# Two transformer layers on one core: spare matmuls behind the opening are left out of the stream of TensorE

## The chip, the core and the metric

The kernel runs on one core of one Trainium2 chip. Five engines work side by side, each through its own list of instructions in order: TensorE (PE in the profile; PEld is its weight load), VectorE (DVE), ScalarE (ACT), GpSimd (POOL) and SyncE (SP), which issues the transfers. They wait for one another through semaphores. The metric is the device time of one execution in microseconds (us); lower is better. The profile also records the share of its full clock that TensorE was granted, and this share is part of the story told here.

## The reference

`x` is 2048 tokens by 512 channels in bf16. The network is attention, MLP, attention, MLP with the same weights twice, each on a layer-normalised input and added back:

```python
def _A_ref(x, wqkv, wo):                       # 32 heads of 16 channels
    q, k, v = ...                              # x @ wqkv, split and reshaped
    scores = einsum("bhqd,bhkd->bhqk", q, k) * 16 ** -0.5
    o = einsum("bhqk,bhkd->bhqd", softmax(scores), v)
    return o.reshape(B, S, D) @ wo
def _B_ref(x, w1, b1, w2, b2):                 # 512 -> 1792 -> 512
    return gelu(x @ w1 + b1) @ w2 + b2

x = x + _A_ref(_layernorm(x), wqkv, wo)
x = x + _B_ref(_layernorm(x), w1, b1, w2, b2)
x = x + _A_ref(_layernorm(x), wqkv, wo)
x = x + _B_ref(_layernorm(x), w1, b1, w2, b2)
```

Per layer there are 32 heads of 2048 by 2048 scores, so the exponentials (134 million per layer) are a large part of the work, and the products have an inner size of only 16.

## The kernel before, in words

**Tiles.** The queries are worked in chunks of 512; a pass is one chunk, a group of heads in four strips of 32 channels, and a run of key tiles of 128. A score cell is one key tile by 512 queries for one strip: a matmul with 32 active rows (two heads, one of them masked to zero in the queries) and 128 columns (L1588, `score`), which lands in one of eight PSUM banks. Up to four cells with different row positions run beside each other in the array.

**Exponentials.** A part of the cells is exponentiated by ScalarE straight out of PSUM, two or three banks in one instruction (L2238, `exps`). PSUM banks 0 to 4 form two slots for it, later six banks: while one slot is read, the other is filled. The rest of the cells goes to VectorE (L1855, `dfirst`), which writes scaled integers; GpSimd (L2101, `shift`) adds constants to them so that the bits read as bf16 are terms of the exponential.

**The product with the values** (L2305, `pvs`): four matmuls of 128 rows by 17 columns beside each other in the array, the 17th column being the row sum, accumulated in bank 6 (`PVB`). A DVE transpose and a division close each pass (L1067 and after).

**Projections and MLP** (L706, `quads`): four matmuls of 32 output columns beside each other. GELU is done by ScalarE in a long instruction over half of the hidden layer (L1267), with a table load before and after.

**The order.** Nothing is scheduled on the chip. At build time, `_Sched.run` plays the whole program through with estimated durations: threads (generators) offer operations, the one that could start first is taken, its instructions are appended to its engine's list (`_Prog.group`), the waits that its reads and writes ask for are put ahead of it (`_dep_waits`), and the engine's planned clock is moved on. `_Prog.emit` then writes the lists out. All engines are therefore in a fixed order, and the durations on the chip only decide how long each wait lasts.

**Spare matmuls.** Before each operation of TensorE, `_Sched.fill` looks at the planned gap up to it. `active` keeps a running mean, over the last 3.4 planned us (`WINDOW`), of how many of four 32-wide strips of the array are at work. As long as the gap holds one more operation and this mean is under 2.3 of 4 (`WARM`), `fill` asks `free` for a PSUM bank that nobody needs at that moment and `filler` for a spare operation: four matmuls of `B2row` with itself (L1576), 512 columns long, written into that bank, whose contents nobody reads; or, into the bank of the open value product, four with zero weights. A spare operation counts 0.213 us in the plan. Its event is kept in `fills`, so that `free` knows that the bank holds nothing of worth.

## Time and profile before

| | us |
|---|---|
| three runs of the kernel | 1415.38, 1415.41, 1416.63 (median 1415.41) |
| the profiled execution, whole | 1417.29 |
| its span, first to last instruction | 1415.4 |
| DVE busy | 1265.5 (89%) |
| ACT busy | 1388.6 (98%) |
| POOL busy | 1006.8 (71%) |

The span is the part of the profiled execution that the trace covers; 1.9 us lie around it. Engine times in the profile are unions of instruction spans. For TensorE such a span contains the pipeline's latency, so that a stretch can look full although the array streams only for part of it; the number of matmuls in a stretch tells more. One instruction of L1576 is one of four matmuls that run beside each other.

A stretch in the table of windows shows: its bounds, its length, the busy time of the engine with the number of instructions in brackets (each one that lies in the stretch at least in part), the granted clock of TensorE as a share of full speed, the mean busy share of the DMA engines, and what they moved in GB/s.

### The profile page before, as it was taken

How to read it: one execution, taken by the hardware profiler on the slowest of the kernel's cores; microseconds unless marked ns; L12 is line 12 of the kernel's file. 1: busy time of each engine (PE TensorE's matmuls, PEld its weight loads, DVE VectorE, ACT ScalarE, POOL GpSimd, SP SyncE). 2: the span in 40 equal slices, each digit the busy share in tenths (PEclk: the TensorE clock that was granted, in tenths of full speed). 3: DMA queues.
4: the chain of work that ended last, by engine and by line, in shares of the span. 5: the costliest groups of instructions: out<-in, count | busy, mean ns of one | idle time of the engine just before them, and what ended most of it. 6: DMA issues, size and time to landing. Idle time of an engine off the chain costs nothing.

```text
span 1415.4 us, 45657 instructions
## 1 busy us (share of the span) xinstructions
PE 1387.9 (98%) x19382; PEld 415.4 (29%) x19382; DVE 1265.5 (89%) x2482; ACT 1388.6 (98%) x1392; POOL 1006.8 (71%) x1257
## 2 busy tenths in 40 slices
PE   8999999999999999999999999999999999999999
PEld 3222222222222222222222222222222222344345
DVE  8999999979999899998998899999888978899884
ACT  7999999999999999999999999999999999999995
POOL 0489778757787678766877779647776776877661
PEclk9999999999999999999999999999999999999999
DMA  5200001123121340214312141101133112311121
GB/s 149 65 2 1 2 2 32 41 89 101 44 54 39 98 106 24 59 41 124 81 39 54 54 121 53 47 16 32 39 102 95 31 35 91 111 17 40 28 72 42
DMA packets 122308, 80.41 MB, mean 57 GB/s; under 512 B 36732, under 2 KB 121084, under 8 KB 122108
## 3 DMA queue, kind: packets, MB, share of 16 engines
q1 hardware_dynamic: 122108, 77.49, 19.7%
q8 instruction: 156, 2.56, 0.7%
q14 instruction: 44, 0.36, 0.1%
HBM read 65.67 MB, written 4.19 MB: 49 GB/s over the span
## 4 chain that ended last, share of the span: by engine, by line
PE 60%; ACT 28%; DVE 9%; POOL 2%; DMA 1%; issue 0%; ACTq 0%; DVEq 0%
ACT pt L2238 24%; PE ps L2305 22%; PE ps L1588 20%; PE ps L706 18%; ACT v L2238 2%; DVE dp L1855 2%; DVE kt L1855 1%; ACT g L1267 1%; ACT q L2238 1%; POOL dp L2101 1%; DVE stats L839 1%; DVE xf L1855 0%; POOL kt L2101 0%; DVE xt L1067 0%; PE ps L1576 0%; DVE xln L870 0%
## 5 line engine op out<-in xcount | busy, mean ns | idle before, releaser
L2238 ACT ACTIVATE pt<-ps 128x1024 bf16<-128x1024 f32 (+1 forms) x1170 | 1160.4, 1123 | 5.5 <-PE ps L1588 4.9
L2101 POOL INT64_ADD dp<-dp x760 | 618.1, 825 | 181.0 <-DVE dp L1855 40.3
L1588 PE MATMUL ps<-qp,kt 32*128 32x512 bf16 x4096 | 543.8, 384 | 9.5 <-ACT pt L2238 4.1
L1855 DVE TENSOR_SCALAR dp<-ps 128x512 uint16<-128x512 f32 x762 | 509.4, 681 | 48.9 <-PE ps L1588 43.8
L1588 PEld LDWEIGHTS ps<-qp,kt 32*128 32x128 bf16 x4096 | 138.8, 91 | 566.5 <-ACT pt L2238 158.4
L2305 PE MATMUL ps<-dp,vc 128*17 128x512 bf16 (+1 forms) x2574 | 288.7, 357 | 0.9 <-POOL xp L2101 0.2
L2305 PE MATMUL ps<-pt,v 128*17 128x512 bf16 (+1 forms) x2810 | 272.7, 359 | 2.5 <-POOL dp L2101 0.7
L2101 POOL INT64_ADD kt<-kt x255 | 205.2, 811 | 89.9 <-DVE kt L1855 43.1
L1855 DVE TENSOR_SCALAR kt<-ps 128x512 uint16<-128x512 f32 x254 | 171.6, 683 | 27.2 <-PE ps L1588 24.7
L706 PE MATMUL ps<-xf,wr 128*32 128x512 bf16 (+1 forms) x1888 | 131.9, 367 | 1.8 <-DMA xf<-xln 1.7
L2305 PE MATMUL ps<-dp,v 128*17 128x512 bf16 (+1 forms) x858 | 123.9, 357 | 3.8 <-DVE xt L1067 2.2
L2305 PE MATMUL ps<-kt,vc 128*17 128x512 bf16 (+1 forms) x948 | 125.1, 340 | 0.3 <-POOL kt L2101 0.2
L2101 POOL INT64_ADD v<-v x111 | 91.5, 831 | 39.2 <-DVE v L1855 18.1
L706 PE MATMUL ps<-wr,g 128*32 128x512 bf16 x1408 | 104.2, 383 | 0.3 <-DMA wr<-in_B_w_dram 0.3
L2305 PEld LDWEIGHTS ps<-dp,vc 128*17 128x17 bf16 x2574 | 77.0, 89 | 66.9 <-issue 34.4
L2101 POOL INT64_ADD xf<-xf x74 | 59.6, 805 | 49.1 <-DVE xf L1855 31.8
L2305 PEld LDWEIGHTS ps<-pt,v 128*17 128x17 bf16 x2810 | 67.7, 88 | 79.8 <-issue 54.2
L1855 DVE TENSOR_SCALAR v<-ps 128x512 uint16<-128x512 f32 x112 | 75.9, 684 | 13.1 <-PE ps L1588 12.0
L1249 DVE TENSOR_SCALAR g<-ps,hb1t 128x512 bf16<-128x512 f32 (+1 forms) x112 | 79.1, 706 | 7.6 <-PE ps L706 7.5
L2305 PE MATMUL ps<-kt,v 128*17 128x512 bf16 (+1 forms) x440 | 68.1, 351 | 0.4 <-DVE v L1063 0.4
L2238 ACT ACTIVATE kt<-ps 128x1024 bf16<-128x1024 f32 (+1 forms) x61 | 59.7, 1057 | 0.1
L2238 ACT ACTIVATE v<-ps 128x1024 bf16<-128x1024 f32 (+1 forms) x55 | 55.6, 1078 | 0.1
(127 smaller groups left out, 1436.7 us busy)
## 6 DMA issues: line engine op xcount, KB each, us to landing
wr<-in_B_w_dram SPq DMA_DIRECT2D x174, 256.0 KB, 2.9
wr<-in_A_wqkv_dram SPq DMA_DIRECT2D x24, 256.0 KB, 3.1
x<-in_A_x_dram SPq DMA_DIRECT2D x7, 512.0 KB, 4.0
wr<-in_A_wo_dram SPq DMA_DIRECT2D x10, 256.0 KB, 3.2
kept<-x SPq DMA_DIRECT2D x4, 512.0 KB, 2.9
x<-kept SPq DMA_DIRECT2D x4, 512.0 KB, 4.1
out_dram<-x SPq DMA_DIRECT2D x16, 128.0 KB, 2.3
q<-in_B_w_dram SPq DMA_DIRECT2D x3, 512.0 KB, 5.0
```

The lines of the kernel that those rows point to most:

```text
L706: return [lambda e, a=a: e.matmul(out[32 * a:32 * a + 32, :], lhsT=lhsT[:, 32 * a:32 * a + 32], rhs=rhs, start=start, stop=stop, tile_posi ...
L839: yield _Op("dve", 0.66, lambda e, t=t, src=src: e.bn_stats(T["STATS"][:, t, :], src), reads=[key], writes=["ST.%d" % t], prio=prio)
L1249: yield _Op("dve", 0.21 + n / 966, lambda e, fc=fc, pb=pb: e.tensor_scalar(T["G"][:, fc, q], pb, T["HB1T"][:, fc:fc + 1], None, op0=ALU.ad ...
L1267: lambda e, g=g: e.activation(out=g, in_=g, func=ACT.Gelu_apprx_tanh), reads=gk, writes=gk, prio=2)
L1588: return (lambda e: e.matmul(o, lhsT=lhsT, rhs=rhs, start=True, stop=True, tile_position=(32 * a, 0)), ["K%d.%d.%d" % (l, gb, kt // 4), "Q ...
L1855: yield _Op("dve", 0.682, lambda e: e.tensor_scalar(u, self.bank(b), E_SCALE, E_BIAS, op0=ALU.mult, op1=ALU.add), reads=["B.%d" % b], writ ...
L2101: op = _Op("pool", PFIX + PWORD * 128 * n * (1 + both), lambda e: e.int64_add(dst, src, by * PACKED), reads=reads, writes=writes)
L2238: yield _Op("act", 0.065 + 0.4267 * n, lambda e, src=src, dst=dst: e.activation(out=dst, in_=src, func=ACT.Exp, scale=0.25), reads=["B.%d" ...
L2305: op.fns.append(lambda e, o=o, lhsT=q[0][0][m], rhs=q[0][1][:, n * m:n * m + n], a=a, st=st, sp=sp: e.matmul(o, lhsT=lhsT, rhs=rhs, start= ...
```

## The change

From a planned time of 60 us on, `fill` does all that it did, but does not append the four matmuls: the waits that they would have needed are still put into TensorE's list, the planned clock still moves on by 0.213 us, and the bank is marked as holding nothing. As the plan's clocks are the same, every later decision is the same too. TensorE's list loses 416 matmuls and nothing else; its waits, and the lists of the other four engines, are unchanged in number and order.

```diff
+FILLED = 60
...
             op = self.filler(b, mode)
             self.mode = mode
-            ev = self.P.group("pe", op.fns, op.reads, op.writes)
-            if b != PVB:
-                self.fills.add(ev)
+            if self.clock["pe"] < FILLED:
+                ev = self.P.group("pe", op.fns, op.reads, op.writes)
+                if b != PVB:
+                    self.fills.add(ev)
+            else:
+                self.P._dep_waits("pe", op.reads, op.writes)
+                ev = None
+                if b != PVB:
+                    self.P.lastw.pop("B.%d" % b, None)
+                    self.P.reads["B.%d" % b] = {}
             self.note(now + into, now + into + MM + cold, op)
             self.ops.append(("pe", now, into + MM + cold, "FILL"))
             self.clock["pe"] = now + into + MM + cold
-            self.end[ev] = self.clock["pe"] + LATENCY["pe"]
+            if ev:
+                self.end[ev] = self.clock["pe"] + LATENCY["pe"]
```

`_dep_waits` writes an engine's waits for the last writers and readers of the named buffers; `lastw` and `reads` are the tables in which those are kept, and clearing a bank in them means that its next user has nothing to wait for on its account.

## The prediction

> **What bounds the kernel now.** I read the page first, then the chain of waits, then the table of windows, then the timeline where the granted clock dips.

> ```profile
> PE 1387.9 (98%) x19382; PEld 415.4 (29%) x19382; DVE 1265.5 (89%) x2482; ACT 1388.6 (98%) x1392; POOL 1006.8 (71%) x1257
> PE 60%; ACT 28%; DVE 9%; POOL 2%; DMA 1%; issue 0%; ACTq 0%; DVEq 0%
> 30.00:1080.00 1050.00, 1036.04 (x13487) 281.84 (x13487) 962.35 (x1846) 1048.36 (x1048) 776.70 (x968) 1.00 0.20 55
> 1095.00:1390.00 295.00, 290.07 (x4905) 106.91 (x4906) 255.76 (x477) 294.64 (x286) 216.08 (x267) 1.00 0.19 53
> ```

> The first two rows show TensorE and ScalarE both at 98%, and the chain that ended last running 60% on TensorE and 28% on ScalarE. The two window rows (PE, PEld, DVE, ACT, POOL in this order) sharpen it: from 30 to 1080 us ScalarE sat idle for 1050 - 1048.36 = 1.64 us, from 1095 to 1390 us for 295 - 294.64 = 0.36 us. So the two engines are tied: whatever delays TensorE soon starves ScalarE, but whatever speeds TensorE up can win back at most those 2.0 us, because ScalarE has no more idle time to give.

> The second thing to see is the clock. This trace holds one dip, and it is an experiment made for us:

> ```profile
> 1082.78:1086.20 3.42, 1.47 (x22) 1.00 0.53 131
> 1086.20:1089.61 3.41, 3.41 (x30) 0.50 0.37 112
> 1089.61:1093.02 3.41, 3.41 (x51) 1.00 0.11 43
> 171.43:174.84 3.41, 3.20 (x35) 1.00 0.03 7
> ```

> ```profile
> 1086.14 1.04 PE L706 MATMUL ps<-xf,wr 128*32 128x512 bf16 x8 [1.73 <-DMA xf<-xln]
> ...
> 1087.65 1.04 PE L706 MATMUL ps<-xf,wr 128*32 128x512 bf16 x8
> ...
> 1090.13 0.39 PE L1588 MATMUL ps<-qp,kt 32*128 32x512 bf16 x3
> ...
> 1091.00 0.39 PE L1588 MATMUL ps<-qp,kt 32*128 32x512 bf16 x3
> ```

> ```profile
> 1087.77 1.02 ACT L2238 ACTIVATE pt<-ps 128x1024 bf16<-128x1024 f32 x1 [2.06 <-PE ps L1588]
> 1089.70 1.94 ACT L2238 ACTIVATE pt<-ps 128x1024 bf16<-128x1024 f32 x2 [0.92 <-PE ps L1588]
> ```

> TensorE waited 1.73 us for a transfer, so the stretch 1082.78 to 1086.20 held only 22 matmuls. In the next 3.41 us it was granted half its clock, then the full clock again. So the clock is judged by stretches of 3.41 us: 22 matmuls were too few, and a stretch of 35 (171.43) kept the clock whole. Somewhere between lies the limit.

> The price: a projection of eight matmuls with a score group of three takes 1087.65 - 1086.14 = 1.51 us at half clock and 1091.00 - 1090.13 = 0.87 us at full clock. A half-clock stretch of a fully loaded TensorE thus does 3.41 / 1.51 x 0.87 = 1.97 us of work and loses 1.44 us. The counts agree: 30 matmuls against 51 right behind, (51 - 30) x 3.41 / 51 = 1.40 us. ScalarE lost 2.06 + 0.92 = 2.98 us over the place, 1.25 us more than the stall of 1.73.

> **The change part by part.** It removes 416 matmuls, and nothing else moves: no DMA, wait or instruction of another engine.

> ```profile
> 60.00:1416.00 1356.00, 33.87 (x416) 1.00 0.19 54
> 239.69:243.11 3.42, 1.22 (x16) 1.00 0.48 80
> 519.58:523.00 3.42, 1.00 (x12) 1.00 0.64 207
> 915.53:918.94 3.41, 1.39 (x24) 1.00 0.01 2
> 918.94:922.36 3.42, 0.52 (x8) 1.00 0.00 0
> 970.14:973.56 3.42, 1.09 (x16) 1.00 0.41 82
> 973.56:976.97 3.41, 0.13 (x4) 1.00 0.02 6
> 1151.05:1154.46 3.41, 2.09 (x32) 1.00 0.02 5
> 1154.46:1157.87 3.41, 2.15 (x40) 1.00 0.00 0
> 1157.87:1161.29 3.42, 0.34 (x8) 1.00 0.00 0
> ```

> These are the windows of L1576 alone. The 33.87 us of span that the spares cover are no saving: nobody reads their banks, and they stand where the plan saw TensorE wait. What they can have delayed is the operation right behind them, and that gain is capped by ScalarE's 2.0 us above. I take 0.6 us, a third, between 0 and 2.0; below nothing it cannot go but through the clock, since no work that remains reads their banks.

> The other side is the clock. The same stretches with all of TensorE's matmuls:

> ```profile
> 239.69:243.11 3.42, 3.02 (x42) 1.00 0.48 80
> 243.11:246.52 3.41, 3.40 (x42) 1.00 0.39 77
> 519.58:523.00 3.42, 3.19 (x40) 1.00 0.64 207
> 523.00:526.41 3.41, 3.41 (x48) 1.00 0.48 140
> 915.53:918.94 3.41, 3.20 (x44) 1.00 0.01 2
> 918.94:922.36 3.42, 3.42 (x46) 1.00 0.00 0
> 970.14:973.56 3.42, 3.08 (x46) 1.00 0.41 82
> 973.56:976.97 3.41, 3.09 (x40) 1.00 0.02 6
> 1151.05:1154.46 3.41, 3.04 (x39) 1.00 0.02 5
> 1154.46:1157.87 3.41, 2.79 (x45) 1.00 0.00 0
> 1157.87:1161.29 3.42, 2.92 (x48) 1.00 0.00 0
> ```

> All are cut on the grid of the dip. Subtract the spares: 239.69 keeps 42 - 16 = 26 matmuls, 519.58 keeps 28, 915.53 keeps 20, 970.14 keeps 30, 1151.05 keeps 7 and 1154.46 keeps 5.

> *Step 1, sure by the row of the dip.* 1151.05 and 1154.46 fall far below 22. ScalarE is in a GELU there and takes no scores:

> ```profile
> 1148.61 6.27 ACT L1267 ACTIVATE g<-g 128x3584 bf16<-128x3584 bf16 x2
> ```

> The clock halves at 1154.46 and stays halved until a busy stretch has passed, to 1161.29. The stretch 1157.87 has 48 - 8 = 40 matmuls to do where 30 fit: 10 x 3.41 / 51 = 0.67 us; the 5 matmuls of 1154.46 take 5 x 0.067 = 0.3 us longer. Together 1.0 us, on the path, because ScalarE resumes on these scores.

> *Step 2, by the limit.* A half-clock stretch costs what does not fit behind it: (n - 30) x 3.41 / 51, n being the matmuls of the next stretch, nothing if n is under 30, at most 1.4. So 239.69 costs nothing (26 follow in 243.11, which at half clock are a full stretch and keep the next one whole); 519.58 costs 18 x 0.067 = 1.2 us; 915.53 (38 follow) 0.54; 970.14 (36 follow) 0.40. The mean is 0.54; two of the stretches not shown have followers as full as 1089.61, so I take 0.65 us, between 0 and 1.4.

> How many there are hangs on the limit between 22 and 35. I measure it against a stretch that streams without a break:

> ```profile
> 1154.03 0.83 PE L1576 MATMUL ps<-b2row 128*32 128x512 bf16 x12
> ...
> 1155.20 1.48 PE L1576 MATMUL ps<-b2row 128*32 128x512 bf16 x24
> ```

> Twelve more matmuls took 0.65 us, so 3.41 us hold 63 at most. I take half of that, 31, as the limit: an estimate that lies inside the bracket. On this grid eleven stretches with 512-column matmuls, the first 239.69 and the last 970.14, hold 20 to 30 without spares; two of them are covered, as 243.11 is, by a dip that the stretch before them set off. So nine dips, 9 x 0.65 = 5.9 us. Three more low stretches after 1235 us mix in 256-column matmuls, where the count misleads; they stay in the upper range.

> The sum: + 1.0 + 5.9 - 0.6 = + 6.3 us. The profiled execution took 1417.29 us (span 1415.4), 1.9 above the median of 1415.41; the sum carries over, so **1421.7 us**. No row says where the grid lies in another execution; the count is for one position of it.

> [...]

> **The rivals.**

> *Few dips (0.32).* The limit lies just above 22, so 26 to 30 matmuls keep the clock. Then step 1 and 915.53 remain at most: + 1.0 + 0.5 - 0.6 = + 0.9, at least + 0.4: 1415.8 to 1416.3 us. For it: the only row of a dip is at 22 with a pause of 1.73 us, and without spares most pauses are shorter. Against: nothing between 22 and 35 was seen whole either.

> *Many dips (0.16).* The limit lies just under 35: some sixteen dips, with the three after 1235 us, at 0.9: + 14.4 + 1.0 - 0.6 = + 14.8, 1430 us.

> *TensorE gains (0.04).* Spares stand in the chain of waits:

> ```profile
> by line: PE ps L2305 32.7%; PE ps L1588 27.1%; ACT pt L2238 18.5%; PE ps L1576 8.7%; PE ps L706 5.5%; DVE dp L1855 3.5%; POOL xp L2101 3.1%; issue 1.4%; DVE nmr L854 0.9%; DVE ry L858 0.7%; PE ps L2313 0.1%
> 239.69:243.11 3.42, 3.42 (x4) 1.00 0.48 80
> ```

> The first row is the chain from 230 to 250 us: 8.7% of 20 us is 1.7 us of spares right ahead of scores. If TensorE alone set the pace there, and at two like places, the kernel would gain 5 us: 1410. It decides from the point at which ScalarE has idle time to follow; the second row, ScalarE's own window, has it busy for 3.42 of 3.42 us at the same place. So the cap of 2.0 us holds, and with no dip beyond step 1 the result would be + 1.0 - 2.0 = 1414.4, slightly faster.

> That the change does nothing is ruled out but for the size: 416 instructions are gone.

> **How the numbers follow.** Forecast (limit about 31; five to ten dips, + 3 to + 10 us) 0.48, few dips 0.32, many 0.16, gain 0.04. The range 1415.6 to 1429 leaves out the lower third of few dips, the gain and the upper half of many dips, about 0.2. A measurement of this kernel can tell some 0.2%, 2.8 us, from no change: under 1412.6 is faster (0.02), over 1418.2 slower. Same holds few dips, half of the gain and a little of the forecast: 0.36. Slower: 0.62.

> **What would show it.** In the changed kernel's windows, stretches of 3.41 us at 0.50 behind the low stretches named; each lowers the mean granted clock by 0.5 x 3.41 / 1415 = 0.0012. ScalarE's waits for L1588, beside each dip, should grow by about 1 us in all where the follower is full. The stretch at 1151 must dip: if it does not, the whole reading of the clock is wrong. If dips come and ScalarE's waits do not, step 2's price is wrong; if 915.53 (20) keeps its clock, the limit is not a count of matmuls. If the time falls by more than 2 us, the tie between the two engines is not what the first rows say.

## The result

The changed kernel took 1424.7 us (median of 4 runs, 1424.33 to 1426.52) against 1415.39 us of the kernel before (4 runs): 1.0072 times as long, interval 1.006 to 1.0085, that is 9.3 us slower by the medians. The ratio is not the quotient of the two medians, which is 1.0066; by the ratio the loss is 10.2 us. The forecast was 1421.7 us, 6.3 us slower.

In the profile of the changed kernel the lines of the code stand nine further down: L2247 is the exponential on ScalarE (L2238 before), L1597 the scores (L1588), L2314 the product with the values (L2305), L715 the projections (L706). First the page's rows and the mean granted clock:

```profile
span 1422.9 us, 44846 instructions
PE 1374.4 (97%) x18966; PEld 407.9 (29%) x18966; DVE 1266.4 (89%) x2482; ACT 1390.5 (98%) x1392; POOL 1007.3 (71%) x1257
PE 59%; ACT 30%; DVE 9%; POOL 1%; issue 1%; ACTq 0%; DVEq 0%
```

```profile
core 0: 1422.9 us, clock 0.987
```

ScalarE runs the same 1392 instructions in a span 7.5 us longer, and 416 matmuls are gone. The number that moved is the clock. A half-clock stretch of 3.41 us costs 0.5 x 3.41 / 1422.9 = 0.0012 of the mean, so 0.987 means some eleven of them. The table of windows of TensorE, cut on the grid of this execution, finds them:

```profile
633.71:637.13 3.42, 1.67 (x27) 1.00 0.27 77
637.13:640.54 3.41, 3.41 (x30) 0.50 0.02 5
640.54:643.95 3.41, 3.41 (x29) 0.50 0.00 0
643.95:647.37 3.42, 3.42 (x63) 1.00 0.42 119
917.02:920.43 3.41, 1.93 (x21) 1.00 0.01 2
920.43:923.85 3.42, 3.08 (x20) 0.50 0.02 5
923.85:927.26 3.41, 3.41 (x27) 0.50 0.00 0
934.09:937.50 3.41, 2.09 (x26) 1.00 0.02 5
937.50:940.91 3.41, 3.41 (x29) 0.50 0.00 0
954.57:957.98 3.41, 2.38 (x29) 1.00 0.00 0
957.98:961.39 3.41, 1.94 (x21) 1.00 0.00 0
961.39:964.81 3.42, 3.17 (x24) 0.50 0.02 5
964.81:968.22 3.41, 3.27 (x29) 0.50 0.19 38
968.22:971.63 3.41, 3.41 (x30) 0.50 0.00 0
1155.95:1159.37 3.42, 1.70 (x15) 1.00 0.00 0
1159.37:1162.78 3.41, 0.63 (x5) 0.50 0.00 0
1162.78:1166.19 3.41, 2.99 (x24) 0.50 0.00 0
1166.19:1169.61 3.42, 3.42 (x32) 0.50 0.02 5
1169.61:1173.02 3.41, 3.41 (x53) 1.00 0.00 0
237.77:241.18 3.41, 2.33 (x31) 1.00 0.19 38
241.18:244.59 3.41, 2.61 (x31) 1.00 0.38 77
244.59:248.00 3.41, 2.46 (x26) 1.00 0.19 38
```

There are five dips with eleven stretches: two at 637, two at 920, one at 937, three at 961, three at 1159. They lie on one grid: between the starts of the dips (637.13, 920.43, 937.50, 961.39 and 1159.37) are 283.30, 17.07, 23.89 and 197.98 us, which are 83, 5, 7 and 58 stretches of 3.41 us (283.30 / 83 = 3.413). Read the busy column ahead of each: 1.67, 1.93, 2.09, 1.94 and 1.70 us of 3.41 let the clock fall; 2.33, 2.38, 2.46 and 2.61 held it. Then read on: in four of the five dips the clock does not return after one stretch as at 1086 in the kernel before. At 920.43, 961.39, 964.81, 1159.37 and 1162.78 the half-clock stretch was itself not full (3.08, 3.17, 3.27, 0.63, 2.99), and the next stayed at half. Of the six full ones five were followed by full speed; 637.13 is the exception, full by this column and yet followed by another half.

What it costs shows on ScalarE, whose own windows over the same places are these, behind a GELU at 635 and in the dips:

```profile
643.95:647.37 3.42, 0.88 (x1) 1.00 0.42 119
920.43:923.85 3.42, 2.64 (x3) 0.50 0.02 5
923.85:927.26 3.41, 2.32 (x3) 0.50 0.00 0
961.39:964.81 3.42, 3.05 (x4) 0.50 0.02 5
964.81:968.22 3.41, 2.61 (x4) 0.50 0.19 38
968.22:971.63 3.41, 2.44 (x3) 0.50 0.00 0
1166.19:1169.61 3.42, 2.10 (x3) 0.50 0.02 5
```

Idle: 2.54 + 0.78 + 1.09 + 0.37 + 0.80 + 0.97 + 1.32 = 7.9 us. ScalarE's waits say the same in one row, the changed kernel's first and the kernel before's second (total, number, longest); the last row is TensorE's wait for the late transfer in the kernel before:

```profile
ACT pt L2247 <- PE ps L1597: 10.2, 16, 2.7
```

```profile
ACT pt L2238 <- PE ps L1588: 4.9, 6, 2.1
...
PE ps L706 <- DMA xf<-xln: 1.7, 1, 1.7
```

Of the 4.9 us before, 2.98 belonged to the transfer that was late at 1085 us and its dip; in the changed kernel's profile no such wait for xf occurs. So 10.2 - (4.9 - 2.98) = 8.3 us are new; the idle time at the dips, 7.9 us, is nearly all of that.

A second measure, which the texts below use, is the delay: how much later the changed kernel's profile starts the same instruction of ScalarE. It is 2.7 us behind the dip at 637 and 8.5 us behind the one at 961 (972.14 against 963.62 us). It falls to 5.4 us where the kernel before had its late transfer, and grows to 7.4 us behind the GELU. That makes 8.5 us for the eight stretches of the first four dips and 2.0 us for the three at the GELU, 10.5 us in all.

### The profile page after: what moved, and what is told of

Its sections match the earlier page's. It is cut to its first block, busy times and chain, and to the rows that moved or that the text cites. A ratio compares the mean times of both kernels' runs of the same rounds, so it can differ in the third digit from the quotient of the medians.

```text
span 1422.9 us, 44846 instructions
## 1 busy us (share of the span) xinstructions
PE 1374.4 (97%) x18966; PEld 407.9 (29%) x18966; DVE 1266.4 (89%) x2482; ACT 1390.5 (98%) x1392; POOL 1007.3 (71%) x1257
## 4 chain that ended last, share of the span: by engine, by line
PE 59%; ACT 30%; DVE 9%; POOL 1%; issue 1%; ACTq 0%; DVEq 0%
ACT pt L2247 24%; PE ps L2314 22%; PE ps L1597 19%; PE ps L715 18%; ACT v L2247 3%; DVE dp L1864 2%; ACT q L2247 1%; ACT g L1276 1%; DVE kt L1864 1%; POOL dp L2110 1%; DVE stats L848 1%; DVE xf L1864 1%; DVE xt L1076 0%; DVE xln L879 0%; DVE v L1007 0%
## 5 line engine op out<-in xcount | busy, mean ns | idle before, releaser
L2247 ACT ACTIVATE pt<-ps 128x1024 bf16<-128x1024 f32 (+1 forms) x1170 | 1162.2, 1119 | 11.1 <-PE ps L1597 10.2
L1597 PE MATMUL ps<-qp,kt 32*128 32x512 bf16 x4096 | 548.1, 387 | 18.2 <-ACT pt L2247 9.2
L1597 PEld LDWEIGHTS ps<-qp,kt 32*128 32x128 bf16 x4096 | 138.7, 91 | 578.4 <-issue 165.7
L2314 PE MATMUL ps<-dp,vc 128*17 128x512 bf16 (+1 forms) x2574 | 293.5, 362 | 1.4 <-ACT pt L2247 0.4
L2314 PE MATMUL ps<-pt,v 128*17 128x512 bf16 (+1 forms) x2810 | 275.3, 361 | 6.6 <-ACT pt L2247 2.4
L2314 PE MATMUL ps<-dp,v 128*17 128x512 bf16 (+1 forms) x858 | 126.2, 362 | 9.7 <-DVE xt L1076 5.6
L715 PE MATMUL ps<-xf,wr 128*32 128x512 bf16 (+1 forms) x1888 | 131.3, 365 | 0.3
L2314 PE MATMUL ps<-kt,vc 128*17 128x512 bf16 (+1 forms) x948 | 127.5, 344 | 2.2 <-POOL kt L2110 0.7
L715 PE MATMUL ps<-wr,g 128*32 128x512 bf16 x1408 | 104.2, 383 | 0.1
L2314 PEld LDWEIGHTS ps<-dp,vc 128*17 128x17 bf16 x2574 | 77.2, 89 | 69.6 <-issue 37.4
L2314 PEld LDWEIGHTS ps<-pt,v 128*17 128x17 bf16 x2810 | 67.7, 88 | 84.6 <-issue 56.0
L2314 PE MATMUL ps<-kt,v 128*17 128x512 bf16 (+1 forms) x440 | 69.3, 356 | 1.7 <-DVE v L1072 1.2
L2247 ACT ACTIVATE kt<-ps 128x1024 bf16<-128x1024 f32 (+1 forms) x61 | 59.7, 1058 | 0.1
L2247 ACT ACTIVATE v<-ps 128x1024 bf16<-128x1024 f32 (+1 forms) x55 | 55.7, 1079 | 0.1
```

Source lines behind the costliest of these rows:

```text
L715: return [lambda e, a=a: e.matmul(out[32 * a:32 * a + 32, :], lhsT=lhsT[:, 32 * a:32 * a + 32], rhs=rhs, start=start, stop=stop, tile_posi ...
L1597: return (lambda e: e.matmul(o, lhsT=lhsT, rhs=rhs, start=True, stop=True, tile_position=(32 * a, 0)), ["K%d.%d.%d" % (l, gb, kt // 4), "Q ...
L2247: yield _Op("act", 0.065 + 0.4267 * n, lambda e, src=src, dst=dst: e.activation(out=dst, in_=src, func=ACT.Exp, scale=0.25), reads=["B.%d" ...
L2314: op.fns.append(lambda e, o=o, lhsT=q[0][0][m], rhs=q[0][1][:, n * m:n * m + n], a=a, st=st, sp=sp: e.matmul(o, lhsT=lhsT, rhs=rhs, start= ...
```

## The experiments

All ten kernels come from the changed one; the waits, the planned clocks and the other four engines' lists stay as they are. The common edit numbers the 125 spare operations (four matmuls each behind the opening) and asks a rule whether one is written out:

```diff
-            if self.clock["pe"] < FILLED:
+            self.nfill += 1
+            if KEEP(self.nfill):
```

Times are medians with a ratio to the kernel before, run in turns on the same chip; where ratio and medians differ, the ratio and its interval decide. The kernel before has dips of its own: of its 28 runs beside the first four kernels, most lay from 1413.6 to 1415.8 us at a granted clock of 1.000, and the seven above 1416.5 were all under 1.000.

**Spares kept in three places only** (635, 909 to 973 and 1150 us; 184 matmuls out).

```diff
-FILLED = 60
+KEEP = lambda n: n <= 21 or 48 < n <= 53 or 57 < n <= 93 or 94 < n <= 111
```

> The spares stay in the three places where the clock fell in the profile of the changed kernel (the GELU at 1150 us, 68 matmuls; 635 us, 20; 909 to 973 us, 144) and before 60 us; the other 184 are left out. Theory, the clock alone: no half-clock stretch there, the delay of 10.5 us that built up at the five dips is gone, the time is within 1 us of the kernel before, 1414.4 to 1416.4 us, perhaps 0.3 us less for the freed TensorE. Rival, each removed spare costs its even share (9.3 us / 416 = 0.022 us per matmul, by what its absence does to the work around it): 184 x 0.022 = + 4.1 us, 1419.5 us.

Measured: 1418.24 us against 1414.82, ratio 1.0024 (1.0012 to 1.0037). More than the theory's nothing, and the even share's + 4.1 us lies inside the interval (+ 1.7 to + 5.2). The profile shows what the theory had missed:

```profile
239.71:243.12 3.41, 1.83 (x26) 1.00 0.38 77
243.12:246.54 3.42, 2.97 (x23) 0.50 0.38 77
246.54:249.95 3.41, 3.35 (x26) 0.50 0.02 5
```

A dip that the changed kernel's profile did not have: there the grid cut the same work at 241.18 and 244.59, into 2.61 and 2.46 us; here it cut at 239.71 and left 1.83. My list of places was taken from one position of the grid.

**Single drops.** Each leaves out the spares of one place alone:

```diff
-FILLED = 60
+KEEP = lambda n: not 94 < n <= 111
```

> Only the 68 spares at the GELU (1150 us) are left out. Theory, the clock: one dip of two to three stretches with TensorE idle in the first, + 2.0 us as in the profile of the changed kernel (delay 5.4 to 7.4 us over 1160 to 1167), + 1.2 to + 2.8 by the place of the grid. Rival, even share: 68 x 0.022 = + 1.5 us. Second rival, my prediction's price of 1.0 us with one stretch only.

Measured: 1416.21 us, ratio 1.0016 (1.0006 to 1.0027). The clock fell behind a stretch with seven matmuls, and stayed down for three (10.24 us); this is TensorE there:

```profile
1151.99:1155.40 3.41, 1.27 (x7) 1.00 0.00 0
1155.40:1158.81 3.41, 1.06 (x5) 0.50 0.00 0
```

The theory's place and length are right; the time alone doesn't tell its price from the even share or from the prediction's 1.0 us, which all lie inside the interval (+ 0.8 to + 3.8). The profiled execution, at 1420.36 us the second longest of the eleven, also has a late transfer and a dip at 1087 us; these occur in the kernel before as well.

```diff
-FILLED = 60
+KEEP = lambda n: not 48 < n <= 53
```

> Only the 20 spares at 635 us are left out. Theory, the clock: the stretch keeps some 20 matmuls, the clock falls and stays down for two stretches since each holds under the limit even when full of half-clock work, + 2.7 us (the step of the delay at 645 us). Rival, even share: 20 x 0.022 = + 0.4 us. My prediction's reading of one half-clock stretch: + 1.4 us at most.

Measured: 1415.55 us, ratio 1.0005 (0.9995 to 1.0015): not the + 2.7 us. The profiled execution had no dip there:

```profile
632.61:636.02 3.41, 2.27 (x30) 1.00 0.27 77
```

The stretch held 2.27 us of work where the changed kernel's held 1.67. The same gap, cut at another point, falls or holds. In 5 of 11 runs the mean granted clock was under 1.000, against 7 of 28 of the kernel before, so these runs do not tell how often the place dips.

```diff
-FILLED = 60
+KEEP = lambda n: not 57 < n <= 93
```

> Only the 144 spares between 909 and 973 us are left out. Theory, the clock: three dips of one to three stretches, + 5.8 us (the delay grows from 2.7 to 8.5 us there). Rival, even share: 144 x 0.022 = + 3.2 us. If the three single drops and the kept one add up to the whole change, the places do not help or hurt each other: 2.0 + 2.7 + 5.8 = 10.5 us, against 9.3 measured for the whole.

Measured: 1419.51 us, ratio 1.0034 (1.0019 to 1.0049), dips at 919 and 960 (two stretches each) and 980 in its profile, and one at 1093, where the late transfer of the kernel before came again. By the median + 4.7 us, above the even share's 3.2; but the interval (+ 2.7 to + 6.9) holds both the even share and the theory's 5.8, and the dip at 1093 is none of this edit's doing.

**What the clock counts.** Every spare operation stays, but with one matmul of 32 columns instead of four beside each other:

```diff
-                ev = self.P.group("pe", op.fns, op.reads, op.writes)
+                ev = self.P.group("pe", op.fns[:4 if self.nfill <= 21 else 1], op.reads, op.writes)
```

> Every spare operation stays, but each behind 60 us is one matmul of 32 columns instead of four beside each other: 312 matmuls fewer, the array as long under way. What does the clock count? If the time in which the array streams, whatever its width: no dip beyond those of the kernel before, 1414.0 to 1416.0 us. If matmuls (or the share of the array at work): the low stretches gain a quarter of what they had, for instance 20 + 6 = 26 at 915 us and 7 + 8 = 15 at the GELU, so most dips of the changed kernel come back, 1418 to 1423 us.

Measured: 1414.74 us against 1414.77, ratio 0.9998 (0.9989 to 1.0006), the granted clock 1.000 in all eleven runs. Its profile at the GELU:

```profile
1147.43:1150.84 3.41, 3.03 (x21) 1.00 0.00 0
1150.84:1154.25 3.41, 2.75 (x15) 1.00 0.00 0
```

Fifteen matmuls held the clock. The counterpart keeps all four matmuls and moves 128 columns in place of 512:

```diff
+            rhs = rhs if self.s.clock["pe"] < 60 else rhs[:, 0:128]
...
+            if self.s.clock["pe"] >= 60:
+                o = o[:, 0:128]
```

> Every spare operation stays with its four matmuls, but each moves 128 columns instead of 512: as many matmuls as in the kernel before, a quarter of the streaming time. If the clock counts streaming time: the dips of the changed kernel come back in most places, 1418 to 1424 us. If it counts matmuls: no dips, 1414 to 1416 us. Rival to the clock altogether (the spares help by keeping TensorE's queue fed, so that the next weights are loaded): same as the kernel before, whatever the granted clock shows.

Measured: 1417.45 us, ratio 1.0024 (1.0013 to 1.0035), the granted clock 0.992 to 0.998 in its twelve runs. By the median it lies just under the range for streaming time, by the ratio (+ 3.4 us) at its lower end; a quarter of that time was kept. The profile is of the shortest of the twelve runs and has one dip. Its first two rows show the fall; the other two, a half-clock stretch behind which the clock came back and another place that held, are used further down:

```profile
1148.95:1152.37 3.42, 2.17 (x51) 1.00 0.00 0
1152.37:1155.78 3.41, 2.19 (x24) 0.50 0.00 0
1155.78:1159.20 3.42, 3.14 (x32) 0.50 0.00 0
633.54:636.95 3.41, 2.05 (x44) 1.00 0.28 77
```

Fifty-one matmuls in one stretch, as many as the loaded 1089.61 of the kernel before had, and the clock fell; fifteen held it. So in these two kernels the clock followed neither the number of matmuls nor how much of the array was at work: one matmul of 512 columns in place of four kept it at 1.000, four with a quarter of the columns left it at 0.992 to 0.998. The time in which the array streams fits both. The rival of a fed queue falls too: here the queue was fed with as many matmuls as before, and the kernel was slower all the same (ratio 1.0024).

**Places and doses.** The three places and 235 to 246 us kept, 136 matmuls out:

```diff
-FILLED = 60
+KEEP = lambda n: n <= 21 or 25 < n <= 37 or 48 < n <= 53 or 57 < n <= 93 or 94 < n <= 111
```

> As the version that kept the spares at 635, 909 to 973 and 1150 us, with the 48 between 235 and 246 us kept too; 136 are left out. That version was 3.4 us slower than the kernel before, and its profile had one dip of two stretches at 243 us (+ 1.9 us). Theory, the clock: that dip is gone and with it 2 to 3.4 us, 1414.8 to 1416.5 us; what is left comes from low stretches at 294, 519 and 1240 to 1270 us where the grid falls badly. Rival, even share: 136 x 0.022 = + 3.0 us, 1417.8 us.

Measured: 1415.07 us, ratio 1.0000 (0.9991 to 1.0009), clock 1.000 in all eleven runs. The even share falls: 136 matmuls cost nothing, and the 48 decide.

```diff
-FILLED = 60
+KEEP = lambda n: n <= 21 or n % 2 == 0
```

> Behind 60 us every second spare operation is left out, 208 matmuls. Theory, a limit on streaming at some 0.43 of a stretch: half of the spares lifts nearly all low stretches over it (20 + 12 = 32 at 915 us, 20 + 10 = 30 at 635 us); only the GELU stays near it. + 0 to + 2.5 us. Rival, even share: half of the whole change, + 4.7 us.

Measured: 1416.94 us, ratio 1.0008 (0.9999 to 1.0018), clock mostly 0.998. Its profile dips at 1154 us, at the GELU, and nowhere else inside the work. The theory's 0.43 is an estimate; by the count of streaming time given further down it lies between two stretches of the changed kernel's profile, the fullest that lost the clock (934.09, 0.41 of its time) and the emptiest that kept it (954.57, 0.46). Half the matmuls gone cost less than half of the loss: the interval ends at 1.0018, and half of 1.0072 would be 1.0036. That is a limit, not a share.

```diff
-FILLED = 60
+KEEP = lambda n: not 25 < n <= 37
```

> Only the 48 spares between 235 and 246 us are left out. My reading so far: the version without them and 136 others lost 3.4 us, the one with them and without the 136 nothing. So these 48 alone should cost it: + 2 to + 3.5 us, the granted clock at 0.996 to 0.998 (one dip of two stretches or a little more). If the clock stays at 1.000 and the time too, the 48 and the 136 were only slow together, and the count of places must be drawn up anew. Even share: 48 x 0.022 = + 1.1 us.

Measured: 1418.10 us against 1414.85, ratio 1.0018 (1.0009 to 1.0027), all eleven runs with a clock of 0.996 to 0.999. The 48 spares alone cost it, + 2.5 us by the ratio, inside what was expected. Its profile shows one dip, behind a stretch that the busy column would have called safe:

```profile
244.29:247.70 3.41, 2.43 (x25) 1.00 0.21 43
247.70:251.11 3.41, 3.41 (x29) 0.50 0.00 0
```

```diff
-FILLED = 60
+KEEP = lambda n: n <= 21 or 25 < n <= 37 or 48 < n <= 53 or 57 < n <= 93 or 94 < n <= 111
...
+                ev = self.P.group("pe", op.fns[:4 if self.nfill <= 21 else 1], op.reads, op.writes)
```

> The least that I expect to keep the clock: spares only before 60 us, at 235 to 246, 635, 909 to 973 and 1150 us, and one matmul of four in each; 346 of the 416 matmuls gone. If streaming time in these places is all that the spares are for: no dips, 1414.0 to 1415.8 us, same as the kernel before. If TensorE gains anything from the matmuls that are gone, up to 0.6 us less.

Measured: 1414.61 us against 1414.85, ratio 0.9998 (0.9989 to 1.0007). With 346 of the 416 matmuls gone the kernel is as fast as before, and not faster. No version beat the kernel before.

**The account.** The four places dropped singly add up to 0.0016 + 0.0005 + 0.0034 + 0.0018 = 0.0073; the whole change measured 0.0072. Each of the four has an interval of 0.0009 to 0.0015 to either side, so that the close match is partly chance. In the changed kernel's profile the delay of 10.5 us comes with eleven half-clock stretches, 0.95 us each. And over the 193 executions whose clock is on record (the changed one, these ten kernels and the kernel before beside them), a straight line through time and mean granted clock (correlation 0.87) gives 0.84 us per 0.001 of clock: 0.84 x 1.2 = 1.0 us for a half-clock stretch of 3.41 us. The line is a correlation and not a price by itself: the 84 runs of the kernel before alone give 2.5 us per 0.001, and in the one dip of it that was profiled a late transfer had held TensorE up as well.

**Where the limit lies.** The busy column doesn't give it: 2.05 us held above and 2.43 us fell. An estimate of the streaming time does better. Count each matmul of 512 columns from its start for 0.217 us (twelve more, three groups of four, took 0.65 us), shorter ones in proportion, twice as long at half clock. In the twelve profiles, from 30 us on and without the last 8 us, sixteen full-clock stretches lost the clock; fifteen of them streamed for 0.19 to 0.42 of their time, and every stretch from 0.46 up held it but one, the 244.29 above with 0.48.

## Why the prediction was right, and where it was not

*What bounds the kernel, and the price of a half-clock stretch at full load (1.25 to 1.44 us)*: right in kind; in this kernel's dips a stretch costs about 1.0 us. That TensorE has some slack where it dips would explain the difference; it wasn't tried.

*Step 1, the GELU at 1151*: it dipped as said. I took one loaded stretch, 1.0 us. It stayed at half clock for 10.24 us, the delay over it grew by 2.0 us, and the drop by itself measured a ratio of 1.0016, 2.3 us by it (0.8 to 3.8, which still holds the 1.0).

*Step 2, nine dips of one stretch at 0.65 us, 5.9 us in all*: two errors in the same term that partly cancelled. There were four such dips in the profile, not nine, but they held eight stretches: the sentence that the half-clock stretch behind 239.69 would be "a full stretch and keep the next one whole" is the step that failed. Stretches at half clock with 3.08 to 3.27 of 3.41 us busy were followed by another. The delay over the eight is 8.5 us, so a dip cost 2.1 us and not 0.65, and the 5.9 of the sum came too low. The forecast had eleven half-clock stretches in all (nine, and two at the GELU) and eleven came, but in five dips and not in ten: that agreement is luck. By the delay the terms are 2.0 and 8.5 us and no gain, 10.5 us in this one execution, where the forecast had 1.0, 5.9 and 0.6 off.

*The limit, half of 63 matmuls*: the wrong measure, and so is the advice ahead of the prediction that the number of matmuls tells more than the busy time. 51 matmuls lost the clock and 15 kept it. In the changed kernel's profile the busy time separates the two: 2.09 us and less fell, 2.33 and more held. In the other profiles it does not, and the streaming time does, but for one stretch. That 243.11 and its neighbour were low at all was right, but whether such a place dips hangs on where the grid cuts it, as the two cuts at 240 us show; the text said so of its count and then used it.

*The gain of 0.6 us on TensorE*: not seen. Both versions that left out 136 and 346 matmuls and kept the clock stand at 1.0000 and 0.9998, 1.3 us to either side; 0.6 us can be neither seen nor excluded at that width. ScalarE's lack of idle time was the right reason for a small cap.

*The rivals.* Many dips, 1430 us: too many, sixteen stretches against eleven. Gain: refuted. Few dips: refuted by the five dips and the ratio. That most pauses without spares are shorter than the 1.73 us of the first dip was no reason for it: at 920 the clock fell behind a stretch that was busy for 1.93 of 3.41 us, and this row of TensorE has its longest pause, 0.61 us:

```profile
920.36 0.59 PE L1597 MATMUL ps<-qp,kt 32*128 32x512 bf16 x3 [0.61 <-ACT pt L2247]
```

What stays open: the limit to better than the estimate above, why 244.29 fell without the 48 spares, why 637.13 was followed by a second half, and what sets the position of the grid. An experiment that fixes that position wasn't tried.

## What to carry to other kernels

In these runs spare work on TensorE was worth keeping where a stretch of 3.41 us would otherwise have streamed for less than about 0.45 of its time (estimated above: 0.19 to 0.42 fell, 0.46 and up held but one of 0.48): not for the array but for its clock, and one narrow matmul at a time did as well as four (ratio 0.9998). Look for the dips in windows of 3.41 us and in the mean granted clock; in the 40 slices of the changed kernel's page (row PEclk) the five dips leave two 8s among the 9s. Judge such a change over several executions, since here the same gap dipped or not by where the grid cut it (busy for 1.67 of 3.41 us and 2.27 at 635 us), and reckon with dips of more than one stretch: here they lasted for one to three, 3.41 to 10.24 us.

## What was not expected of the hardware

The width of a matmul plays no part that these runs show: one of 32 columns in 128 kept the clock as well as four (1.000 in all eleven runs), with 312 matmuls fewer in the whole kernel.
